# Whole-head stores of 2 MB and a last V load in halves, in a decode attention kernel with its gradients

## The chip, the cores and the metric

One core of one Trainium2 chip. The metric is device time in microseconds (us) of one execution, median over runs. Runs lie within 0.2% of the median for the kernel before. The rounds ran on four different chips, so times are compared by their ratio to the kernel before in the same round. "MB" in the title and "2 MiB" in the text are the same transfers: 128 partitions of 16 KB.

## The reference, cut to what matters

```python
B, H, Sq, Skv, Dh = 1, 32, 1, 8192, 128          # bf16

def forward(q, k, v):
    scores = einsum('bhqd,bhkd->bhqk', q, k) * Dh ** -0.5
    attn = softmax(scores)
    return einsum('bhqk,bhkd->bhqd', attn, v)

out, vjp = jax.vjp(forward, q, k, v)
return out, *vjp(grad_out)                        # out, dq, dk, dv
```

There is one query per head. K and V of a head are 2 MiB each and have to be read; dK and dV are 2 MiB each and have to be written. Everything else is small. 32 heads make 268 MB of traffic. dK is an outer product of the vector dS (8192) with q (128), dV one of the probabilities p with the output gradient.

## The kernel before

K and V of a head lie as 128 partitions of 64 rows. All DMAs are issued by SP, in program order:

```python
NST = 2                                            # stores per head and tensor
def rows_of(x, h, c, parts):                       # part c of a head in HBM
    L = NT // parts
    return x[0, h].rearrange("(p n) d -> p n d", p=P)[:, c * L:(c + 1) * L, :]

def load_v(h):                                     # V has 2 tiles, K has 3
    Vt[h] = vpool.tile([P, NT, D], BF16, tag="V", name="Vt")
    parts = NCH if h in (0, H - 1) else 1          # NCH = 4
    for c in range(parts):
        nc.sync.dma_start(slots(Vt[h], c, parts), rows_of(v, h, c, parts))

def outer(h, which, r):                            # quarter r of dK or dV
    if r == 0:
        x[which] = gpool.tile(...)                 # 2 tiles each for dK and dV
    nc.vector.tensor_tensor(...)                   # 1.22 us on VectorE
    parts = 4 if h == H - 1 else NST
    if r % (4 // parts) == 4 // parts - 1:
        c = r // (4 // parts)
        nc.sync.dma_start(rows_of(dst, h, c, parts), slots(G, c, parts))

for h in range(H + 1):                             # p_ = h - 1
    # K stage of head h: DVE transposes of K, 64 score matmuls (k_scores)
    # load_v(h + 1)
    # dS of p_, dK quarters 0..3 of p_ spread over the softmax of head h,
    #   dQ of p_ (64 matmuls); load_k(h + 2) after the second quarter
    # V stage of head h: 64 transposes of V, output (64 matmuls), dP (64 matmuls)
    # dV quarters 0..3 of h
    ...
```

(Comments stand for code that is cut.) So SP issues in a head: V, dK half, K, dK half, dV half, dV half.

## Time and profile before

| | before |
|---|---|
| median, first measurement | 668.13 us (668.04 to 668.19) |
| span of the profiled run | 667.0 us |
| TensorE, VectorE, ScalarE busy | 77%, 77%, 27% |
| mean traffic | 405 GB/s |
| packets | 29807 |

No compute engine is busy all the time. The DMA issues, part 6 of the profile page, have as columns: what moves, the issuing queue, the number of issues, the size of each, and the median time from issue to landing:

```profile
Kt<-in_k_dram SPq DMA_DIRECT2D x31, 2048.0 KB, 28.0
out_dram<-G_dv SPq DMA_DIRECT2D x62, 1024.0 KB, 25.8
out_dram<-G_dk SPq DMA_DIRECT2D x62, 1024.0 KB, 28.0
Vt<-in_v_dram SPq DMA_DIRECT2D x30, 2048.0 KB, 28.3
Vt<-in_v_dram SPq DMA_DIRECT2D x8, 512.0 KB, 13.8
```

Loads of 2 MiB and stores of 1 MiB take about the same 26 to 28 us. That is time in a queue, not time of moving.

### The profile page before, as it was taken

The page shows a single profiled execution, that of the slowest core. Times are in us where ns is not written, and L with a number is a line of the kernel's source. Part 1 is how long each engine was busy: PE and PEld are TensorE (multiplying, and loading weights), DVE is VectorE, ACT ScalarE, POOL GpSimd, SP SyncE. Part 2 cuts the span into 40 slices and gives each one's busy share as a digit, 9 for nine tenths or more (in the row PEclk, how much of TensorE's full clock was granted, in tenths as well). Part 3 has the DMA queues.
Part 4 walks back from the last instruction along what each step waited for, and adds up shares of the span by engine and source line. Part 5 has one row for each costly group of instructions (what it writes and reads, how often), then busy time and mean ns, then how long its engine had stood idle before and what let it go on. Part 6 is the DMA issues. An engine that isn't in the chain of part 4 may idle for free.

```text
span 667.0 us, 23105 instructions
## 1 busy us (share of the span) xinstructions
PE 516.8 (77%) x10727; PEld 485.8 (73%) x10727; DVE 512.5 (77%) x658; ACT 182.1 (27%) x321; POOL 0.7 (0%) x6
## 2 busy tenths in 40 slices
PE   2887988888887777878779787787776888778881
PEld 1887878878877767877668676677766777677870
DVE  4797888888877797777877778777788776887762
ACT  0333323232323222232222322223312223223230
POOL 0000000000000000000000000000000000000000
PEclk9995556566565565555555655666557665555555
DMA  8999999999999999999999999999999999999783
GB/s 330 414 425 424 419 427 414 424 423 426 425 425 424 425 425 424 425 429 423 423 427 426 423 416 422 413 412 418 395 423 418 397 416 406 409 420 403 270 357 142
DMA packets 29807, 269.94 MB, mean 405 GB/s; under 512 B 3472, under 2 KB 3472, under 8 KB 6032
## 3 DMA queue, kind: packets, MB, share of 16 engines
q1 hardware_dynamic: 29712, 268.48, 97.0%
q8 instruction: 83, 1.36, 0.7%
q14 instruction: 12, 0.10, 0.0%
HBM read 134.23 MB, written 134.23 MB: 403 GB/s over the span
## 4 chain that ended last, share of the span: by engine, by line
DMA 75%; PE 17%; DVE 3%; ACT 2%; issue 1%; SPq 0%; ACTq 0%
DMA Kt<-in_k_dram 26%; DMA Vt<-in_v_dram 26%; DMA out_dram<-G_dv 23%; PE T_ps L168 7%; PE s_ps L145 2%; PE dp_ps L185 2%; PE m_ps L185 2%; PE dp_ps L180 1%; DVE XK_sb L133 1%; ACT XT_sb L170 1%; PE m_ps L255 1%; DVE G_dk L195 1%; PE m_ps L268 1%; PE s_ps L161 0%; ACT qd L211 0%
## 5 line engine op out<-in xcount | busy, mean ns | idle before, releaser
L168 PE MATMUL T_ps<-ident,Vt 128*128 128x128 bf16 x2048 | 228.7, 302 | 31.9 <-DMA Vt<-in_v_dram 31.9
L168 PEld LDWEIGHTS <-Vt 128*128 128x128 bf16 x2048 | 201.1, 142 | 33.8 <-DMA Vt<-in_v_dram 33.6
L133 DVE STREAM_TRANSPOSE XK_sb<-Kt 128x1024 f32<-128x1024 f32 x128 | 148.2, 1213 | 81.1 <-DMA Kt<-in_k_dram 81.1
L170 ACT COPY XT_sb<-T_ps 128x1024 f32<-128x1024 f32 x128 | 129.5, 1012 | 189.7 <-PE T_ps L168 189.7
L195 DVE TENSOR_TENSOR G_dk<-ds_rep,qd 128x2048 bf16<-128x2048 bf16 x128 | 155.7, 1219 | 1.1
L195 DVE TENSOR_TENSOR G_dv<-p_rep,qd 128x2048 bf16<-128x2048 bf16 x128 | 148.2, 1220 | 8.5 <-ACT p_rep L277 8.5
L180 PEld LDWEIGHTS <-XT_sb 128*128 128x128 bf16 x2048 | 74.7, 106 | 27.2 <-ACT XT_sb L170 27.2
L180 PE MATMUL dp_ps<-doT,XT_sb 128*128 128x1 bf16 x2048 | 73.6, 166 | 24.4 <-ACT XT_sb L170 24.4
L145 PE MATMUL s_ps<-q_blk,XK_sb 128*128 128x4 bf16 x2048 | 59.1, 168 | 23.2 <-DVE pdt L216 20.5
L145 PEld LDWEIGHTS <-XK_sb 128*128 128x128 bf16 x2048 | 56.5, 103 | 25.5 <-DVE pdt L216 22.3
L185 PE MATMUL dp_ps<-ds_rep,Kt 128*128 128x1 bf16 x2048 | 64.7, 165 | 6.6 <-issue 6.0
L185 PEld LDWEIGHTS <-Kt 128*128 128x128 bf16 x2048 | 59.9, 104 | 12.3 <-issue 12.3
L185 PEld LDWEIGHTS <-Vt 128*128 128x128 bf16 x2048 | 61.1, 105 | 0.0
L185 PE MATMUL m_ps<-p_rep,Vt 128*128 128x1 bf16 x2048 | 60.5, 166 | 0.0
L226 ACT COPY dq_all<-dp_ps 128x1 f32<-128x1 f32 x32 | 5.1, 159 | 173.9 <-PE dp_ps L185 173.9
L268 PEld LDWEIGHTS m_ps<-rs,ones_f 128*128 128x128 f32 x64 | 16.0, 310 | 48.6 <-ACT e L267 48.6
L268 PE MATMUL m_ps<-rs,ones_f 128*128 128x1 f32 x64 | 18.7, 360 | 39.2 <-ACT e L267 39.2
L264 DVE TENSOR_REDUCE nbias<-m_ps 128x1 f32<-128x128 f32 x32 | 9.3, 292 | 22.0 <-ACT qd L211 22.0
L255 PE MATMUL m_ps<-diag,ones_f 128*128 128x128 f32 x64 | 25.3, 499 | 0.7 <-DVE diag L253 0.7
L218 DVE SCALAR_TENSOR_TENSOR ds_rep<-dp_ps,pdt,p_s 128x256 bf16<-128x256 f32 x32 | 15.5, 484 | 12.0 <-PE dp_ps L180 9.6
L277 ACT ACTIVATE p_rep<-e,rinv 128x256 bf16<-128x256 f32 x32 | 16.2, 507 | 30.3 <-DVE rinv L275 30.3
L211 ACT CAST qd<-m_ps 128x256 bf16<-128x256 f32 x32 | 11.9, 372 | 42.4 <-PE m_ps L207 42.4
(40 smaller groups left out, 163.0 us busy)
## 6 DMA issues: line engine op xcount, KB each, us to landing
Kt<-in_k_dram SPq DMA_DIRECT2D x31, 2048.0 KB, 28.0
out_dram<-G_dv SPq DMA_DIRECT2D x62, 1024.0 KB, 25.8
out_dram<-G_dk SPq DMA_DIRECT2D x62, 1024.0 KB, 28.0
Vt<-in_v_dram SPq DMA_DIRECT2D x30, 2048.0 KB, 28.3
Vt<-in_v_dram SPq DMA_DIRECT2D x8, 512.0 KB, 13.8
Kt<-in_k_dram SPq DMA_DIRECT2D x4, 512.0 KB, 5.4
out_dram<-G_dv SPq DMA_DIRECT2D x4, 512.0 KB, 16.9
out_dram<-G_dk SPq DMA_DIRECT2D x4, 512.0 KB, 10.7
```

The source lines that it names most:

```text
L133: nc.vector.transpose(XK[h][:, :, :, u, :], slots(Kt[h], u, NCH).rearrange("p g d -> p (g d)").bitcast(F32).rearrange("p (g w j) -> p g w ...
L145: nc.tensor.matmul(out[:, g, :], lhsT=cols[:, g, c // 2, c % 2], rhs=q_blk[:, h, c, :], start=(c == 0), stop=(c == 2 * NB - 1), skip_group ...
L168: nc.tensor.transpose(T_ps[:, i, :], Vt[h][:, c * CH + i, :], ident[:])
L170: nc.scalar.copy(X.rearrange("p c s -> p (c s)").bitcast(F32), T_ps.rearrange("p c s -> p (c s)").bitcast(F32))
L180: nc.tensor.matmul(st[h]["dp"][:, n:n + 1], lhsT=X[:, i, :], rhs=doT[:, h:h + 1], start=True, stop=True, skip_group_check=True)
L185: nc.tensor.matmul(out_col, lhsT=Xt[:, n, :], rhs=rep[:, n, 0:1], start=(n == 0), stop=(n == NT - 1), skip_group_check=True)
L195: nc.vector.tensor_tensor(slots(G, r, 4).rearrange("p n (a b) -> p n a b", b=R), slots(rep, r, 4).unsqueeze(2).to_broadcast([P, Q, D // R, ...
L211: nc.scalar.copy(x["qd"][:].rearrange("p a d -> p (a d)"), x["m"][:, 256:512])
L218: nc.vector.scalar_tensor_tensor(out=x["ds"][:], in0=x["dp"][:, 0:NT].unsqueeze(2).to_broadcast([P, NT, R]), scalar=pdt[:], in1=x["p_s"][: ...
L255: nc.tensor.matmul(x["m"][:, 128:256], lhsT=ones_f[:], rhs=diag[:], start=True, stop=True, skip_group_check=True)
L268: nc.tensor.matmul(x["m"][:, 0:1], lhsT=ones_f[:], rhs=rs[:], start=True, stop=True, skip_group_check=True)
L277: nc.scalar.activation(x["p"][:], e[:].unsqueeze(2).to_broadcast([P, NT, R]), ACT.Copy, scale=rinv[:])
```

## The change

The intent: fewer, larger transfers. A store of a head goes out whole after its fourth quarter; head 0 keeps halves so that the first stores start early, head 31 keeps quarters so that the last ones end early. The last V load comes in two parts instead of four. The K load is only rewritten and moves the same parts.

```diff
-NST = 2
+NST = 1
...
     def load_k(h):
-        parts = NCH if h == 0 else 1
-        for c in range(parts):
-            nc.sync.dma_start(slots(Kt[h], c, parts), rows_of(k, h, c, parts))
+        if h == 0:
+            for c in range(NCH):
+                nc.sync.dma_start(slots(Kt[h], c, NCH), rows_of(k, h, c, NCH))
+        else:
+            nc.sync.dma_start(Kt[h][:], rows_of(k, h, 0, 1))
...
     def load_v(h):
-        parts = NCH if h in (0, H - 1) else 1
+        parts = NCH if h == 0 else 2 if h == H - 1 else 1
...
     def outer(h, which, r):
-        parts = 4 if h == H - 1 else NST
+        parts = 4 if h == H - 1 else 2 if h == 0 else NST
```

SP's order in a head becomes: V, K, dK, dV.

## The prediction

> **What bounds the kernel now.** I read the strip of slices first, then the chain that ended last, the waits of SP's queue, and the trace's records of single DMA packets and semaphore increments.
>
> ```profile
> DMA  8999999999999999999999999999999999999783
> GB/s 330 414 425 424 419 427 414 424 423 426 425 425 424 425 425 424 425 429 423 423 427 426 423 416 422 413 412 418 395 423 418 397 416 406 409 420 403 270 357 142
> ```
>
> The DMA engines are full from the first slices to the 37th of 40; TensorE and VectorE are each busy 77% of the span. The last three slices are not full: 270, 357 and 142 GB/s. That looks like a tail to be won, and the second part of the change (last V load in halves) is aimed at it. The chain says what steady state is made of:
>
> ```profile
> 184.97 27.97 DMA Kt<-in_k_dram
> ...
> 213.00 25.79 DMA out_dram<-G_dv
> ...
> 238.86 28.31 DMA Vt<-in_v_dram
> ...
> 267.24 27.99 DMA Kt<-in_k_dram
> ...
> 295.29 25.81 DMA out_dram<-G_dv
> ```
>
> Columns: start, length, what. Nothing but transfers. One round (K, dV, V) is 82.3 us and covers four heads, 20.57 us a head. A head moves 8 MiB = 8.39 MB; at the 425 GB/s of the strip that is 19.7 us. Why 20.57? And why does a transfer take 26 to 28 us when 1 or 2 MiB need 2.5 or 4.9? The second has a plain answer in the waits of SP's queue from 200 to 400 us:
>
> ```profile
> SPq L203 <- DMA Kt<-in_k_dram: 44.9, 10, 4.5
> SPq L75 <- DMA Vt<-in_v_dram: 44.8, 10, 4.5
> SPq L203 <- DMA out_dram<-G_dk: 42.0, 19, 2.4
> ```
>
> A store (L203) has no data from a K load, yet it waits for one. The trace shows the DMAs going round eight semaphores, so that the ninth waits for the landing of the first: at most eight are under way. A head has six (two loads, four stores), so eight are 8/6 x 20.57 = 27.4 us of traffic, which is the time to landing.
>
> The first question is answered by the semaphore increments, of which each of these DMAs gets sixteen. Their spread, first to last, is 0.8 us for the K load that lands at 19.5 us, 4 us at 95 us, 7.6 us at 160 us, 15 us at 300 us and 20 to 21 us from 380 us on. The last increment is 7 to 9 us behind the fifteenth from 310 to 390 us: one engine is slower than its fellows and falls further behind. From last increment to last increment (25 heads, 100 to 610 us) it needs 4.91 us for each 2 MiB load but 2.65, 2.67, 2.64 and 2.92 us for the four 1 MiB stores. The earliest engine's medians between 100 and 250 us are 4.86 and 2.45. The slow one's intervals add up to 663.8 us over the whole execution, with no hole in it: it ends its last store at 665.4 us and has work at every moment. Its dV parts issued at 640 land at 656.7 to 660.5 us. **So the bound is neither the mean rate nor the tail of computation, but one DMA engine that is slow in stores.** The low rate in the last slices (and the 413 GB/s of 400 to 610 us) is the other engines running out of issued work while this one is 12 to 20 us behind.
>
> **What the Trainium skill says.** "DMA: Bandwidth & Descriptors", section "Why a DMA increments its semaphore by 16 and not by 1": each engine taking part adds one after its own data, and only the full sixteen mean that all has landed. The spreads above agree and make the slowest engine decide. The same page, "Latency and other measured facts", says that engines 7 and 15 are usually slower than the others in traces, with an uncertain cause; the trace has one slow engine, unnumbered in what I can read. Its "Rules for kernel authors" ask for 1 MiB or more per DMA. Both kernels' main transfers obey that, so no large gain is to be had from that rule: on the fast engine 1 MiB stores already go at 2.45 us, half of a 2 MiB load's 4.86. The section "Anatomy of one DMA" gives about 2 us fixed cost per DMA, for GpSimd's path. With eight queued it does not appear here: back-to-back stores land 2.45 us apart on the fast engine.
>
> **The change, part by part.**
>
> Part 1, stores of 2 MiB for heads 1 to 30: 60 stores of two halves become 60 single ones. A partition's row in one packet is then 16 KB, not 8 KB. Packets in the steady state show 309 ns (8 KB, median) and 611 ns (16 KB, loads, median), each starting 3 ns before its predecessor's end. One engine carries 8 rows: a pair of halves is 16 x 306 = 4896 ns, plus two semaphore packets of a net 5 ns; one whole store is 8 x 608 = 4864 plus 5. The difference is 37 ns, times 60 = **2.2 us**.
>
> On the slow engine there is more at stake. Its stores cost 2.65 + 2.67 + 2.64 + 2.92 = 10.88 us a head where 4 x 2.45 = 9.80 would be the fast engine's: an excess of 1.08 us a head, 33 us over the kernel. How much depends on packets or on DMAs? I followed its packets for some stores: they are not 309 but 314 to 399 ns, at places locked to the phase of the head; the dV half in which TensorE runs the K scores and dQ has nearly all packets at 370 to 390. Packets under way while SP issues another DMA are among the slow (the fourth of a dK half, 361 to 385). The first packet of a load is 634 to 667 ns instead of 611. The last 512 KiB stores, after TensorE is done, take 1.22 to 1.28 us: no excess. Something else takes turns with this engine as time passes, most while other engines run many instructions; it does not look like a price per packet. I therefore let most of the excess stand and take off only what goes with an issue or with a switch from store to load: two issues and one switch fewer per head. An issue is worth some 60 ns (361 to 385 against 320), a switch 45 ns (655 against 611): 2 x 0.06 + 0.045 = 0.165 us a head, times 30 = 5.0 us, of which I count two thirds, as the phase moves too: **3.3 us**.
>
> Issue order also moves. Before: V, dK half, K, dK half, two dV halves. After: V, K, dK, dV. With four DMAs a head eight semaphores span two heads, 40 us, so the wait of SP for an old landing should vanish (it is 10 x 4.5 us of two kinds in 200 us). This saves nothing by itself, because the slow engine already has 20 us of work in front of it.
>
> Part 2, V of head 31 in two parts instead of four: two semaphore packets, nothing in bytes. It frees SP, which issued the four over 10.65 us from 611 us while finished dK waited until 626.5 us. But the slow engine came to that dK only at 639 us. Worth **0.1 us**.
>
> The rewritten K load moves the same parts: 0. Head 0 keeps halves and head 31 quarters, so start and last stores stay as they are.
>
> Sum: 2.2 + 3.3 + 0.1 = 5.6 us. 668.1 - 5.6 = **662.5 us**.
>
> **Rivals.**
>
> (a) The excess is a price per packet or per store. Then halving both takes half of 33 us, about 16: 652. If 2 MiB stores went like loads on this engine (4.91), it would be 10.88 - 9.82 = 1.06 us a head, 32 us: 636. For it: its loads, with 16 KB packets, show almost no excess. Against: the phase locking, and the 4 KB stores at the end without any.
>
> (b) The tail is the bound and the freed issue shortens it. Slices 38 to 40 moved 270, 357 and 142 GB/s; filled at 425, their loss is 155 + 68 + 283 = 506 GB/s x 16.7 us = 8.4 MB, 20 us: 648. Against it stands that the last increments have no hole there. Conversely, computation sets a floor: V of head 30 lands at 619.0 us and the last dK block is done at 654.7, some 36 us later, plus about 4 us for the last store and the small outputs; the slow engine needs 46.7 us from that V to its end. The floor lies 6 to 7 us lower, so up to that much can be gained before it bites.
>
> (c) A whole-head store holds its G buffer (two of each kind) until all 2 MiB have landed, and starts only after the fourth block. In ring order dV of head h lands one load (4.9 us) before V of head h+2, near which dV of h+2 is computed: slack 3 us or so. dK of h lands about 4 us before its buffer is wanted. Before, no wait of VectorE for a store is listed. If these slacks fail, VectorE stalls, loads go out later, and if that eats the 20 us of backlog I would see 668 to 680.
>
> (d) Nothing: both sizes are long enough, and the excess moves along with the phase: 666 (2.2 us alone).
>
> **Range and chances.** Most weight lies between (d) and my sum plus a little more from the excess: 658 to 666. Rival (a) or (b) in full or half gets 13%; a new wait 8%, but seldom 2% in size (13 us). So 652 to 667 for 8 in 10; faster by over 2% (under 654.8) 0.13, within 2% 0.85, slower 0.02.
>
> **What would show it.** Period of a head in the chain: 20.35 to 20.45 us if right; 20.0 if half of the excess goes; 19.5 for all of it. SP's waits for K and V landings gone from stores; time to landing of loads above 28 us. Last increments still unbroken to the end. 8 KB packets gone but for head 0 and the last V, 16 KB stores near 611 ns on most engines, and still stretched on the slow one. I am wrong if VectorE waits for stores of G, if the spread of the increments shrinks to a few us, or if the slow engine has holes: then the bound was another.

## The result, and the profile after

The kernel after takes **673.46 us** (671.30 to 674.87, 4 runs) against 668.09 us of the kernel before: ratio 1.0078, 95% interval 1.0051 to 1.0106. Ratios here are the mean time of one kernel's fast runs over that of the other's fast runs of the same rounds, so not quite the ratio of the medians. That is slower beyond the noise; the predicted 662.5 us and the range of 652 to 667 us were wrong.

The DMA strip of the profile after (40 equal slices):

```profile
DMA  8999999999999999999999999999999999999663
GB/s 334 412 424 425 429 421 431 421 428 426 423 428 426 428 423 427 426 425 428 425 428 422 427 427 427 411 419 406 381 428 386 423 411 392 390 405 402 286 262 141
DMA packets 20878, 269.93 MB, mean 402 GB/s; under 512 B 2480, under 2 KB 2480, under 8 KB 4528
```

Up to the 25th slice it is about as before. From the 26th to the 37th four slices fall to 381 to 392 GB/s, where before none was under 395. 30% of the packets are gone.

From 200 to 400 us SP's queue no longer waits for landings. Its waits there (who waited for whom, us in total, times, longest):

```profile
SPq L77 <- PE dp_ps L187: 56.0, 10, 7.4
SPq L83 <- PE T_ps L170: 54.2, 9, 6.8
SPq L205 <- DVE G_dv L197: 49.9, 10, 5.0
SPq L205 <- DVE rinv L277: 26.4, 10, 2.7
```

These are waits for tiles to be free and for blocks to be computed: each DMA now goes out as soon as its data allow. The time to landing did not fall for it, it rose:

```profile
Kt<-in_k_dram SPq DMA_DIRECT2D x31, 2048.0 KB, 30.7
Vt<-in_v_dram SPq DMA_DIRECT2D x30, 2048.0 KB, 31.4
out_dram<-G_dv SPq DMA_DIRECT2D x30, 2048.0 KB, 33.2
out_dram<-G_dk SPq DMA_DIRECT2D x30, 2048.0 KB, 33.0
```

The chain that ended last from 280 to 400 us (start, length, what; its nine longest pieces) shows V as what is waited for:

```profile
276.23 31.55 DMA Vt<-in_v_dram
307.82 1.89 PE T_ps L170 x16
...
317.40 31.79 DMA Vt<-in_v_dram
349.24 1.89 PE T_ps L170 x16
...
359.19 31.37 DMA Vt<-in_v_dram
390.60 1.89 PE T_ps L170 x16
```

Two heads take 41.4 us (307.82, 349.24, 390.60), 20.7 us a head. VectorE waits for no store: among its waits are only loads and other engines. So the head's period did not shrink from 20.57 to the predicted 20.35 to 20.45 us.

**Where the time came from.** Each DMA here ends in sixteen semaphore increments, one of each DMA engine, and the trace has the time of each. The last of the sixteen minus the last of the DMA in front of it is what that DMA cost the slowest engine. (The landing times in the prediction are 0.3 us early against the page's clock; intervals are not touched by that.) In both kernels these intervals leave no hole, so their sum is the time. By kind, in us:

```
            K      V      dV     dK     sum
before    159.8  159.2  174.7  169.2   662.9
after     164.6  158.1  176.8  167.7   667.2
           +4.8   -1.1   +2.1   -1.5    +4.3
```

The spans of the two profiled runs differ by 4.4 us. The stores, from which the prediction expected 5.5 us, cost 0.6 us more. The K loads cost 4.8 us more, 4.1 us of it late: K loads issued from 250 to 400 us take the slowest engine 4.85 us before and 4.91 us after, those issued from 400 to 610 us 4.96 and 5.37. The median spread between first and last increment late in the run is 20.8 us before and 24.9 us after.

### The profile page after: what moved, and what is told of

It is laid out like the page before. It is cut to its first block, busy times and chain, and to the rows that moved or that the text cites.

```text
span 671.4 us, 22983 instructions
## 1 busy us (share of the span) xinstructions
PE 514.6 (77%) x10727; PEld 484.8 (72%) x10727; DVE 511.2 (76%) x658; ACT 182.1 (27%) x321; POOL 0.7 (0%) x6
## 4 chain that ended last, share of the span: by engine, by line
DMA 57%; PE 36%; ACT 2%; DVE 2%; issue 1%; SPq 0%; ACTq 0%
DMA Vt<-in_v_dram 56%; PE T_ps L170 20%; PE m_ps L187 5%; PE dp_ps L182 3%; PE s_ps L147 2%; PE dp_ps L187 2%; ACT XT_sb L172 1%; PE m_ps L286 1%; PE m_ps L257 1%; PE m_ps L270 1%; DVE G_dk L197 1%; DMA Kt<-in_k_dram 1%; DVE XK_sb L135 1%; ACT e L269 0%; PE s_ps L163 0%
```

## The experiments

Two questions: why did the stores not get cheaper, and why did the late K loads get dearer? All ratios are against the kernel before of the same rounds. Where a run is wrong this is said.

### The two parts of the change, each alone

`e1`: the kernel after, with

```diff
-        parts = NCH if h == 0 else 2 if h == H - 1 else 1
+        parts = NCH if h in (0, H - 1) else 1
```

> Whole 2 MiB stores, last V still in quarters. Theory (the slow DMA engine's stores cost the same per byte in one DMA as in two, and its K loads get slower late in the run because of the deeper queue that whole stores allow): the whole loss comes with the stores, so 672 to 675 us, as the full change; the slow engine's store intervals 5.25 and 5.6 us for 2 MiB, its K loads after 400 us about 5.3 to 5.4 us. Rival (the loss comes from the last V in halves, in the tail): 666 to 668 us.

Measured 671.86 us, ratio 1.0069 (1.0055 to 1.0083). Store intervals of the slowest engine 5.28 (dK) and 5.63 us (dV), late K loads 5.19 us.

`e2`: the kernel before, with the opposite edit of the same line.

> Stores in halves as before, last V in two parts instead of four. Theory: the slow engine has 12 to 20 us of work in front of it when SP is freed, so nothing changes: 667.5 to 668.5 us. Rival (the tail pays for SP's late issue): if issuing the dK halves some 8 us earlier helps, 660 to 665 us; if the halves make the last head wait for V, 670 to 674 us.

Measured 668.21 us, ratio 1.0004 (0.9991 to 1.0017). The loss comes with the whole stores; the last V load is worth nothing either way. So the low rates of the last slices were not a tail that this edit could shorten.

### Order or size?

`e3`: the kernel after, but a store goes out as two halves, both after the fourth quarter.

```diff
+        if parts == 1:
+            if r == 3:
+                for c in range(2):
+                    nc.sync.dma_start(rows_of(dst, h, c, 2), slots(G, c, 2))
```

> The changed kernel, but each whole store as two 1 MiB DMAs issued together after the fourth block: order and time of issue as after the change, packets of 8 KB and six DMAs a head as before. Theory (depth of the queue decides, not the size of the packet): eight DMAs are again 1.33 heads, the spread of the last landing is capped at 20 to 21 us as before and the K loads of the slow engine stay near 4.95 us late in the run: 667 to 670 us. Rival 1 (the order of issue, K before dK and stores side by side, is what costs): 672 to 675 us. Rival 2 (packets of 16 KB are worth 2 us after all, hidden by the loss elsewhere): 2 us above the theory, 670 to 672 us.

Measured 673.19 us, ratio 1.0078 (1.0066 to 1.0091). The theory missed; rival 1 was right about the time. The sizes are those of before, eight DMAs are 1.33 heads again, the spread late in the run is capped at 21.5 us and late K loads are near 5.02 us, as the theory said. Yet the time is that of the change, mainly because the dV halves cost 2.85 and 2.84 us where they had cost 2.64 and 2.92: 178.3 us for all of dV instead of 174.7. **But for the last V load, which `e2` shows to be worth nothing, only order and time of issue differ between this kernel and the one before, and that costs 5 us.**

Set beside the change itself, `e3` also shows size alone, at the same order: all stores together cost 347.9 us in halves and 344.5 us whole, 3.4 us less, while the K loads cost 160.9 and 164.6 us, 3.7 us more (one profiled run each). The saving of whole stores is there, and the dearer K loads eat it.

`e4`: the kernel after with the heads' addresses turned by 16 (wrong).

```diff
-        return x[0, h].rearrange(...)
+        return x[0, (h + H // 2) % H].rearrange(...)
```

> The changed kernel, with the addresses in HBM of K, V, dK and dV turned by 16 heads (heads 16 to 31 first), so that results are wrong on purpose. Theory (loads become slow once the spread of landings has reached its cap and the fast engines run dry and restart together): loads of the fast engines and K of the slow one still become slow only from about 400 us on, and the time stays 671 to 675 us. Rival (the addresses of the later heads are slow): the slow loads appear in the first 300 us and are gone after it.

Measured 672.43 us, ratio 1.0071. The slow K loads stay late (4.90 to 4.92 us before 400 us, 5.27 after). The addresses of the later heads are not the cause.

### What makes one engine slow in stores?

`e5`: the kernel before, with the contractions for the output and dQ cut to their first and last matmul (wrong).

```diff
-        for n in range(first, last):
+        for n in (0, NT - 1):
+            if not first <= n < last:
+                continue
```

> The kernel before with the contractions for the output and dQ cut from 64 matmuls each to 2 in a head (wrong on purpose), so that TensorE runs some 124 of 320 matmul pairs a head less, DMAs unchanged. Theory (the slow engine's stores are stretched by something that goes with the number of instructions that the engines run): the excess of 1.08 us a head falls by a third to a half, above all in the last dV half (2.92 us), total 650 to 658 us. Rival (the engine is slow in stores by itself, or by the issue and descriptors of DMAs): the four halves stay at 2.65 and 2.92 us and the time at 665 to 669 us.

Measured 654.84 us, ratio 0.9807 (0.9793 to 0.9822). No transfer was touched; 13 us went with matmuls on an engine that is 77% busy and was not the bound. The halves cost 2.56, 2.57, 2.49 and 2.76 us instead of 2.65, 2.67, 2.64 and 2.92. The cut also raises the granted TensorE clock (0.65 to 0.67 instead of 0.57 to 0.59) and shifts phases, so by itself it does not single out the number of matmuls; `e11` below gains with the clock unchanged (0.58 to 0.59).

`e6`: the DMAs of the kernel before in their order, with no computation; stores come from a zeroed tile (wrong).

> The DMAs of the kernel before in its order and sizes, with no computation at all (stores come from a zeroed tile; wrong on purpose). Theory: without other instructions no engine is slow in stores; spread of landings stays under 8 us, 1 MiB stores 2.45 us and 2 MiB loads 4.87 us on the last engine too, 19.6 us a head, 630 to 640 us. Rival (the engine is slow by itself): last landings still 2.6 to 2.9 us per 1 MiB store and 655 to 668 us.

Measured 637.29 us, ratio 0.9541. Its strip has no tail:

```profile
span 635.8 us, 257 instructions
...
DMA  8999999999999999999999999999999999999997
GB/s 309 424 429 430 422 432 424 427 433 423 430 425 427 427 428 430 428 429 430 430 427 432 427 430 434 428 430 428 425 430 432 426 431 427 431 432 428 424 427 305
```

The spread stays at 4 us, 1 MiB stores cost 2.46 us on the last engine as on the first. The kernel before thus loses 30 us to something that comes with its computation; as the work of all engines was taken out here, this run does not say whose.

`e10`: the cut of `e5` on the kernel after.

> The changed kernel with the two contractions cut to 2 matmuls each, to be set beside the kernel before with the same cut (654.84 us; wrong on purpose too). Theory: with fewer instructions the slow engine falls behind less, the cap is never reached, the K loads of the last part are not hit and only the saving in packets is left, about 2 us: 651 to 655 us. Rival (the order of the stores costs 4 to 6 us in any case): 658 to 661 us.

Measured 658.16 us, ratio 0.9851. The theory missed again and the rival was right: with few matmuls too the new order costs 3.3 us, with late K loads at 4.91 us (none above 4.94). The stores cost 332.5 us against 330.1 in `e5`, 2.4 us more, and 305 TensorE instructions a head start during them against 233. So the order makes stores dearer by itself.

### The count that explains it

After `e3` and `e5` I counted, for each store issued between 120 and 600 us, the TensorE instructions (matmuls and weight loads) that start while it passes the slowest engine. The interval is taken 0.5 us ahead of the increments; that is a choice, and its effect is told below. Means per store:

```
kernel  store              us     TensorE instructions
before  dK half, first    2.63        59
        dK half, second   2.67        86
        dV half, first    2.64        59
        dV half, second   2.92       201
after   dK whole          5.29       160
        dV whole          5.63       305
e3      dV halves         2.85, 2.84 154, 157
```

Before, from 341.8 to 344.7 us a second dV half passes. What TensorE starts meanwhile (start, us, what, count at the end of the line):

```profile
341.63 1.31 PE L145 MATMUL s_ps<-q_blk,XK_sb 128*128 128x4 bf16 x44
342.81 0.99 PE L185 MATMUL dp_ps<-ds_rep,Kt 128*128 128x1 bf16 x32
343.73 0.44 PE L161 MATMUL s_ps<-sm,lane 128*32 128x64 f32 x8
344.10 0.74 PE L185 MATMUL dp_ps<-ds_rep,Kt 128*128 128x1 bf16 x22
```

That is K scores, dQ and the small step between them (L161): 106 narrow matmuls, each with a weight load. After, from 338.1 to 343.8 us a whole dV passes, with all of it:

```profile
...
338.26 0.61 PE L182 MATMUL dp_ps<-doT,XT_sb 128*128 128x1 bf16 x16
339.63 0.58 PE L182 MATMUL dp_ps<-doT,XT_sb 128*128 128x1 bf16 x16 [0.76 <-ACT XT_sb L172]
340.07 1.85 PE L147 MATMUL s_ps<-q_blk,XK_sb 128*128 128x4 bf16 x64
341.78 0.99 PE L187 MATMUL dp_ps<-ds_rep,Kt 128*128 128x1 bf16 x32
342.70 0.44 PE L163 MATMUL s_ps<-sm,lane 128*32 128x64 f32 x8
343.07 0.88 PE L187 MATMUL dp_ps<-ds_rep,Kt 128*128 128x1 bf16 x27
```

Before, the V load behind the dV halves covered the end of dQ, and the loads between the dK halves other parts. Now 461 TensorE instructions a head start during stores of the slow engine instead of 403 (per 4 MiB stored; the means of the table add up to slightly more).

### Putting a load where the matmuls are

If that is the cause, only order needs to change. `e11`: the kernel before, V load issued before the second dV half of the head in front.

```diff
-            if 0 < h < H - 1:
-                load_v(h + 1)          # was: after k_scores(h)
...
         outer(h, "dv", 1)
+        if h + 2 < H:
+            load_v(h + 2)
         outer(h, "dv", 2)
         outer(h, "dv", 3)
```

> The kernel before with only the order of issue changed: the V load is issued before the second dV half of the head in front of it instead of behind it. Theory (what a store costs the slow engine depends on what TensorE runs as it passes; the K scores and dQ, 4.9 to 9 us after K lands, are dense in matmuls; now the second dV half passes there at 2.92 us, with the new order the V load does): the second dV half falls from 2.92 to about 2.65 us, loads stay at 4.9 us, 0.27 us a head, 658 to 663 us. Rival (that half is dear by its address or by its place behind another store): 2.9 us as before, 666 to 669 us. If VectorE or TensorE has to wait for stores or V: over 669 us.

Measured 659.69 us, ratio 0.9884 (0.9868 to 0.9901), correct. The V load passes the slow engine from 338.0 to 343.0 us, and what TensorE starts then is the dense part:

```profile
337.84 1.45 PE L145 MATMUL s_ps<-q_blk,XK_sb 128*128 128x4 bf16 x49
339.15 0.99 PE L185 MATMUL dp_ps<-ds_rep,Kt 128*128 128x1 bf16 x32
340.07 0.44 PE L161 MATMUL s_ps<-sm,lane 128*32 128x64 f32 x8
340.44 1.01 PE L185 MATMUL dp_ps<-ds_rep,Kt 128*128 128x1 bf16 x32
```

The load takes 4.9 us all the same. The dV halves fall to 2.55 and 2.52 us, and 247 instructions a head start during stores. All of dV costs 162.0 us instead of 174.7; dK 172.2 instead of 169.2, as one of its halves now meets the output contraction.

`e12`: the same edit on the kernel after (`load_v(h + 2)` before the fourth dV quarter, so before the whole dV store).

> The changed kernel with the V load issued before the whole dV store of the head in front of it. Theory: the V load, not the dV store, passes during K scores and dQ, so that the dV store falls from 5.62 to 5.3 us or less for 2 MiB, and the packet saving of 2 us shows: 658 to 664 us if the K loads late in the run are still hit as in the changed kernel, less if not. Rival (2 MiB stores side by side are not the point): 671 to 674 us.

Measured **657.67 us** (657.09 to 657.87), ratio 0.9848 (0.9833 to 0.9862), correct. This version beats both kernels. It has 250 instructions a head in stores, as `e11`, and is 2 us faster than that. That is the size of the saving in packets that the prediction gave (2.2 us), but the two orders are only alike, not equal (in `e11` loads pass between the halves), so 2 us is no clean measure of it; `e3` beside the change gives 3.4 us. Against the change, stores are 13.3 us cheaper here and K loads 5.5 us (164.6 to 159.1), V loads 3.5 us dearer. The chain from 280 to 400 us (start, length, what) shows its period, 40.3 to 40.4 us for two heads, 20.2 a head:

```profile
290.41 4.63 DVE XK_sb L135 x4
...
330.78 4.62 DVE XK_sb L135 x4
...
371.11 4.62 DVE XK_sb L135 x4
```

It also has a wait that neither kernel had, VectorE for a dV tile (us in total, times, longest):

```profile
DVE G_dv L197 <- DMA out_dram<-G_dv: 67.5, 21, 3.8
```

`e15` takes it away with a third dV tile (`bufs=3`).

> The fastest version so far (whole stores, V load issued before the dV store; 657.67 us) with a third tile for dV, which takes away VectorE's waits for dV stores (67 us in all). Theory (the slow engine is the bound, and those waits lie beside it): within 1.5 us of that version, 656 to 659 us. Rival (these waits are on the path now): 645 to 654 us.

Measured 658.03 us, ratio 0.9853: the same. 67 us of waits beside the bound cost nothing measurable; the slow engine's intervals are again without a hole.

### The late K loads

`e9`: the kernel after, with a load of 256 bytes behind each V and K load, which only takes up a place among the eight DMAs under way.

```diff
+    def nothing(n):
+        nc.sync.dma_start(nil[:, n, :], q.rearrange("b h s d -> (b h s) d")[0:16, 0:8])
...
                 load_v(h + 1)
+                nothing(2 * h)
...
             load_k(h + 2)
+            nothing(2 * h + 1)
```

> The changed kernel with a 256-byte load behind each V and each K load, so that a head again has six DMAs and eight under way are again 1.33 heads; stores stay whole, packets 16 KB. Theory (whole stores let the fast engines run 24 to 25 us ahead, and late in the run the slow engine's K loads then fall together with loads that all the others start at once): the spread is again capped at 20 to 21.5 us, the K loads of the slow engine after 400 us fall from 5.2 to 5.4 back to about 5.0 us, and the time to 668 to 671 us. Rival (the K loads are slow because of the order of issue): K stays above 5.2 us and the time at 671 to 675 us.

Measured 670.72 us, ratio 1.0039 (1.0026 to 1.0053), within what the theory said. The spread late in the run is 19.4 us; a late K load and the small one before it take 4.74 + 0.20 = 4.94 us together, against 5.37 for the K load alone. So how far the fast engines may run ahead matters for whether late K loads are hit. The trace of the change shows a coincidence besides. Ten of its K loads pass the slow engine between 411 and 608 us, and the other engines are then on the next K load (its median landing comes 0 to 7.5 us later). Seven of the ten took the slow engine 5.10 to 6.06 us, and for these the next K load took the others 5.4 to 6.1 us (median of the sixteen intervals). Three took 4.86 to 4.88 us, and for these it took the others 4.9 us. That the others' restart, after they ran out of work, is what hits the load is argued, not shown. The small loads cost some time themselves.

### Which engine, and which instructions

`e7`: the kernel before, dV stores of six heads cut at partition 120.

> The kernel before with the dV stores of every fifth head (2, 7, 12, 17, 22, 27) each cut into partitions 0 to 119 and 120 to 127. The Trainium skill (DMA: Bandwidth & Descriptors, how many engines) says that 120 partitions go to the 15 lowest-numbered engines and 8 partitions to the lowest 8. Theory (one slow engine bounds the kernel): if it is the sixteenth, it drops 5.6 us of work in each of six heads, its lag falls in steps of that size, and the time falls to 638 to 650 us, until the next slowest engine is the bound. If the slow engine is another one, it gets 0.6 us more in each of those heads and the time is 670 to 673 us. Rival (the bound is the mean rate or the tail, not one engine): 667 to 670 us whichever it is, as the bytes are the same.

Measured 672.72 us (668.81 to 678.21), ratio 1.0080. The trace shows fifteen late increments and one at once for the 120-partition part, and eight late ones for the rest, as the Trainium skill says of a DMA issued by SP ("DMA: Bandwidth & Descriptors", section "Why a DMA increments its semaphore by 16 and not by 1"). The slow engine took part in the first (its last landing came 2.6 to 4.3 us after that of the DMA in front, in the first half of each dV) and up to 390 us not in the second, whose last landing came 1.2 to 3.5 us earlier. So it was not the sixteenth and the run could not gain. From 460 us on the rests land last too, by 0.2 to 0.4 us: another engine, among the eight lowest, is by then as far behind. These eight carry the rests besides (by design 0.3 us more each time), so this does not show a second engine that is slow by itself. That the place differs from run to run is a guess from the unusual scatter.

`e8`: the same with cuts of the second dV half at 126, 117, 108, 121 and 100, one in each of five heads.

> One look. The kernel before, with the second dV half of heads 8, 12, 16, 20 and 24 cut at partition 126, 117, 108, 121 and 100. By the Trainium skill (DMA: Bandwidth & Descriptors, how many engines) the first parts then run on the 14, 13, 12, 11 and 10 lowest-numbered engines (9, 9, 9, 11 and 10 rows each)[...]. Theory (one engine is slow, and the run that left out the sixteenth put it among numbers 8 to 14): where the slow engine takes part, the last landing of the first part comes 2.9 to 4 us after the last one of the DMA in front of it; where it does not, several us before. The place where this changes names the engine. Rival (slowness moves between engines): no single place.

676.74 us. By the rule of the same section the rests of 2, 11, 20, 7 and 28 partitions run on 2, 11, 10, 7 and 14 engines. The last landing came 3.7 to 4.2 us after the one in front in all five first parts, and of the rests the slow engine was in those with 7 to 14 engines and not in that with 2. By the same rule it was thus among the third to seventh here and, up to 390 us, among the ninth to fifteenth in `e7`. `e7` and `e8` ran on different chips, so it is not shown whether its place depends on the chip, the run or the kernel. No single place to spare came out of these runs.

`e13`: the kernel before with 200 one-element memsets a head on GpSimd.

```diff
+        for i in range(200):
+            nc.gpsimd.memset(nil[:, 0:1], 0.0)
```

> The kernel before with 200 memsets of one element a head on the idle GpSimd, which nothing waits for. If an instruction of any engine costs the slow DMA engine's stores some 2.2 ns: 6600 of them, half of them during stores, 7 us: 673 to 677 us. If only TensorE's count: 667 to 669 us. (If they delay VectorE[...], VectorE's means in the profile show it.)

As a time this failed: 973.93 us, because GpSimd itself started a memset only every 147 ns and ended last, alone. But the work proper is in the trace: its last dK store lands at 673.1 us instead of 665.7, 7.4 us later, and VectorE's busy time is unchanged (512.3 and 512.5 us). Some 76 memsets a head fall in stores, and 428 TensorE instructions instead of 403. So instructions of another engine than TensorE go with dearer stores too.

`e14`: the kernel before with 24 one-element matmuls behind each half of dQ.

```diff
         contract(Kt[h], st[h]["ds"], out, half * NT // 2, (half + 1) * NT // 2)
+        for i in range(24):
+            nc.tensor.matmul(st[h]["dp"][0:1, 160:161], lhsT=ident[0:1, 0:1],
+                             rhs=ident[0:1, 0:1], start=True, stop=True, skip_group_check=True)
```

> The kernel before with 24 matmuls of one element by one element behind each half of dQ (96 more TensorE instructions a head, next to no data). Theory (the instruction as such costs): those that start during the second dV half cost 2.2 ns each, with 60 to 96 of them there 0.13 to 0.21 us a head, 671 to 676 us. Rival (the rows that matmuls read are what costs): 667 to 669 us.

Measured 670.09 us, ratio 1.0033 (1.0016 to 1.0050); dQ came out wrong, which was not meant. Between the two expectations. The K stage got longer, and nearly all added instructions started during loads: 421 a head in stores instead of 403. The run is thus inconclusive on whether it is the instruction or the data it reads that counts.

All stores of 1 and 2 MiB issued between 120 and 600 us from the two kernels and twelve of the experiments (all but `e6`, `e7`, `e8`), 986 in number, fit one line:

```
time on the slowest engine = 2.454 us per MiB
                           + 2.4 ns per TensorE instruction that starts meanwhile
                           + 4.7 ns per GpSimd instruction
```

It accounts for 83% of the variance of what goes beyond 2.454 us per MiB. With the interval taken 0 to 1 us ahead the first price stays at 2.3 to 2.6 ns; the second, which rests on `e13` alone, goes from 3.2 to 5.8. The line shows what goes together, not by which path. Rivals that the same stores can test:

- A store right behind another store: 0.03 us dearer if added to the line, and without the count it accounts for 39% only.
- Size: 2 MiB stores come out 0.055 us cheaper than two of 1 MiB, 3.3 us for 60 of them (an estimate from the fit).
- TensorE's busy time in place of its count: 77%. The two go together (correlation 0.97), so the runs hardly tell number from duration.
- Reading of instructions from memory: the traces have it as packets of their own. This is the line of the page of the kernel before (queue, packets, MB, share of 16 engines):

```profile
q8 instruction: 83, 1.36, 0.7%
```

Each of these packets has 16 KB and takes about 960 ns. A store in whose interval one starts is 8 ns dearer, with an uncertainty of 6. So these packets are not what slows the slow engine.

## Why the prediction was wrong

**Right.** The bound is one DMA engine that is slow in stores; its intervals are without a hole in both kernels, and `e6` shows the transfers without that slowness. All signs that the prediction named came true but the period of a head. SP's waits for landings vanished and saved nothing. The last V load in two parts is worth nothing (`e2`). No wait of VectorE for stores came (rival c). The excess is not a price per packet or store (rival a): whole stores kept it, 5.29 + 5.63 = 10.92 us a head against 10.88. The tail is not the bound (rival b). A saving by size is there: predicted 2.2 us; 3.4 us in the stores of the change against `e3`, at the same order, and 2.0 us between `e11` and `e12`, at a similar one. The change itself hides it.

**The step that failed** is the 3.3 us of part 1: "I therefore let most of the excess stand and take off only what goes with an issue or with a switch from store to load". I had seen that the excess is locked to the phase of the head and highest where K scores and dQ run. I allowed for a move of the phase only by taking a third off the gain (5.0 to 3.3 us), and of the new order I reckoned only that SP's wait would vanish. I did not work out which phase the whole stores would meet. It is the order that decides this. The new order put the whole dV store on K scores and dQ: 58 instructions more a head during stores, at 2.4 ns 0.14 us a head, 4.2 us in 30 heads (an estimate from the line above). Less 2.2 us of packets that leaves 2.0 us, less the 3.3 to 3.4 us found for size some 0.8; measured, dV and dK together cost 0.6 us more. In place of -5.5 us for the stores the runs show +0.6.

**A term that was missing** is the late K loads, +4.8 us in the profiled run. The prediction noted that the other engines run ahead and are stopped by the eight DMAs under way, and took that for harmless, since it only makes them idle. With four DMAs a head they get 4 us further ahead, and the slow engine's K loads are then hit late in the run. `e9` takes most of that back, `e4` rules out the heads' addresses; by what path it happens stays open.

What an instruction does to that one DMA engine is also open. Reading of instructions is tested above and is not it, as far as the trace shows it. Writing of the profiler's own records would go by number of instructions too. The record gives a span and a clock for every timed run, so all were profiled, and no run tells whether the slowness is there without the profiler.

## What to carry to other kernels

When transfers are the bound, look at the last of the sixteen increments of each DMA, not at the mean rate: one engine can be 20 us behind while the strip looks full. Before making transfers larger, ask what order they then take on the queue and which part of the computation each will meet; here larger stores alone were worth 2 to 3 us, the order 5 to 16. Waits off that engine's path, even 67 us of them, need no cure.

## What the Trainium skill lacked or had wrong

- "DMA: Bandwidth & Descriptors", the table of latency and other measured facts: it has engines 7 and 15 as the slow ones and guesses at GpSimd's descriptor path. Here all transfers are issued by SP and one engine is slow in stores only (2.64 to 2.92 us for 1 MiB against 2.45), in step with the number of TensorE and GpSimd instructions (2.4 and 4.7 ns each), not at all without computation (2.46), and two looks, on two chips, put it at different places.
- The same page's rule of 1 MiB or more per DMA does not conflict with these runs, but the page has nothing on order: going from 1 to 2 MiB is worth 3.4 us of 668 in the stores (the change against `e3`), moving one load in the order 8.1 us (`e11`) and, with whole stores, 14 to 16 us (`e12` against 671.9 to 673.5).
- No page says that loads can become slow once most engines have run out of work and restart together, as happens here late in the run: 16 KB load packets average 614 to 618 ns in the stretches from 120 to 400 us and 648 to 655 ns from 400 to 600 us in the kernel before, 611 ns from 400 to 600 us in `e6`, where the spread stays at 4 us, and the slow engine's K loads rise to 5.37 us in the kernel after.
